# Attention with transposed scores, no row maximum, and both products in 64-column tile pairs

## The chip, the cores and the metric

One core of one Trainium2 chip runs the kernel; the other cores are idle. The metric is the device time of one execution in microseconds (us), the median of several executions. Executions of one kernel agree closely (the kernel before: 1264.5 to 1266.7 over all its runs here), and all timed runs below are of the fast state. Runs that were looked at once, with one time, are marked so; their state is unknown.

Some terms. TensorE multiplies matrices; VectorE, ScalarE and GpSimd work element by element (the exp is ScalarE's); SyncE here only issues DMAs, the transfers between the large memory and the on-chip one. "Issuing" is the time that SyncE spends on starting a transfer. A packet is the piece that one of the core's 16 DMA engines moves at a time. PSUM is where TensorE's products land; a bank edge, in the prediction below, is column 512 or 1024 of a score buffer there, where the kernel cuts two of a head's score products (`cut` in the diff). A slot is one of the buffers that a group of heads is loaded into.

## The reference

```python
B, H, Sq, Sk, D = 16, 32, 192, 1024, 128           # q, k, v: bf16, normal * 0.05

def reference(q, k, v):
    scale = q.shape[-1] ** -0.5
    scores = jnp.einsum("bhqd,bhkd->bhqk", q, k) * scale
    p = softmax(scores, axis=-1)
    return jnp.einsum("bhqk,bhkd->bhqd", p, v)
```

There are 512 independent heads of 192 queries and 1024 keys. K and V are 134.2 MB each, Q and the output 25.2 MB each: 318.8 MB pass through the DMA engines whatever the kernel computes.

## The kernel before

Scores stand with queries on the partitions. A unit is 128 queries of one head, or the last 64 queries of two heads together, so three units make a pair of heads. Per unit: TensorE makes 128x1024 scores; VectorE finds the row maximum and copies the scores out; GpSimd (two units of three) subtracts the maximum, or ScalarE takes the exp; TensorE transposes the result in 8 blocks; ScalarE copies the transposed block out (taking the exp there for two units of three); TensorE multiplies by V. K and Q arrive transposed by the DMA engines, 16 heads at a time, into two slots.

```python
# SyncE: the loads of a group of G = 16 heads (stores cut)
e.dma_start_transpose(kt[:, s], kf[h0:h0 + G].rearrange("g k d -> (g k) d")).then_inc(sxk[s], 16)
e.dma_start_transpose(qt[:, s], qf[h0:h0 + G].rearrange("g k d -> (g k) d")).then_inc(sxq[s], 16)
...
e.dma_start(vs[:, s], vf[h0:h0 + G].rearrange("g (p t) d -> p g t d", t=KT_TILES)).then_inc(svl[s], 16)

# TensorE, per unit: scores, then the transposes of an earlier unit, then V of a still earlier one
ins = pe.matmul(S[:, cs], qt[:, s, x * SQ: x * SQ + 128], kt[:, s, ...512 columns...], start=True, stop=True)
...
for t in range(KT_TILES):
    ins = pe.transpose(PT[:, t, :], X[:, t: SK: KT_TILES], ident[:])
...
ins = pe.matmul(O[:, sl, :], PTS[:, t, :], vs[:, s, x, t, :], start=first, stop=last, ...)
if with_rs:                                        # row sums: one more column, with the same weights
    ins = pe.matmul(O[:, 3, sl: sl + 1], PTS[:, t, :], ones[:, 0:1], ...)
```

## Time and profile before

The kernel before takes 1265.1 us. First the engines' busy time, the DMA's busy tenths and its GB/s in 40 equal slices of the span, its packets, and the chain of waits (shares of the span, followed back from the last instruction), all from the page of the kernel before:

```profile
PE 1234.2 (98%) x20480; PEld 1009.4 (80%) x20480; DVE 1102.0 (87%) x2304; ACT 1048.6 (83%) x1281; POOL 960.4 (76%) x518
...
DMA  9999999999999999999999999999999999999941
GB/s 288 268 261 240 278 280 266 288 270 245 254 269 261 279 233 255 281 275 262 261 230 272 271 276 268 252 251 272 272 267 281 253 263 252 271 261 281 244 118 27
DMA packets 790743, 321.89 MB, mean 255 GB/s; under 512 B 724992, under 2 KB 724992, under 8 KB 790528
...
PE 97%; SPq 1%; DMA 1%; ACT 0%; issue 0%; DVE 0%; ACTq 0%
```

TensorE (PE) looks like the one bound: busy for 98% of the span, and 97% of the chain. The DMA engines are at nine tenths until the last loads have been issued, although nothing in the chain waits for them. Of 790,743 packets, 724,992 are under 512 bytes.

One microsecond at a time (each line: window, then busy time of each engine, granted TensorE clock, busy share of the DMA engines, GB/s), from the windows of the kernel before:

```profile
643.00:644.00 1.00, 1.00 (x21) 0.81 (x18) 0.95 (x2) 1.00 (x3) 1.00 (x2) 1.00 1.28 290
644.00:645.00 1.00, 1.00 (x25) 1.00 (x24) 0.94 (x1) 0.84 (x2) 1.00 (x1) 1.00 1.33 300
645.00:646.00 1.00, 1.00 (x14) 0.77 (x12) 0.66 (x3) 0.58 (x1) 0.20 (x1) 1.00 1.83 34
646.00:647.00 1.00, 1.00 (x22) 0.59 (x20) 1.00 (x4) 0.86 (x1) 0.75 (x1) 1.00 0.55 120
647.00:648.00 1.00, 1.00 (x21) 0.97 (x20) 0.97 (x3) 1.00 (x2) 1.00 (x1) 1.00 1.28 291
666.00:667.00 1.00, 1.00 (x17) 0.77 (x14) 0.97 (x6) 1.00 (x2) 1.00 (x1) 1.00 1.10 418
667.00:668.00 1.00, 1.00 (x21) 0.81 (x18) 0.95 (x2) 1.00 (x3) 1.00 (x2) 1.00 1.01 385
668.00:669.00 1.00, 1.00 (x25) 1.00 (x24) 0.94 (x1) 0.84 (x2) 1.00 (x1) 1.00 1.06 406
```

At 643 us K is being transposed: 290 GB/s, and this figure does not move. At 645 it falls to 34. The trace's packet records have a fetch of 16 KB of instructions (queue 8) starting at 644.6 us; there are 164 such fetches, one every 7.7 us. At 666 V is being copied, at 385 to 418 GB/s, and a fetch that starts at 666.7 us does not stop it. The packet records give the sizes: K and Q move in packets of 256 bytes, V in packets of 2 KB.

| Before, from the trace | |
|---|---|
| K and Q: 159.4 MB at 290 GB/s (worked out) | 550 us |
| V: 134.2 MB at 390 GB/s, the median of the half-microsecond stretches that hold V alone (worked out) | 344 us |
| last V load issued, by the queue's timeline | 1192 us |

### The profile page before, as it was taken

To read this page: it belongs to the slowest core of one execution; us is meant where nothing else is said; L and a number is where in the kernel's file an instruction comes from. 1 tells how busy PE (TensorE), PEld (TensorE's weight loads), DVE (VectorE), ACT (ScalarE), POOL (GpSimd) and SP (SyncE) were. 2 spreads that over 40 slices of the span, in tenths; PEclk is the share of its full clock that TensorE was granted. 3 is DMA by queue.
4 is the path that set the end of the run, shared out by engine and by line. 5 is a ranking of instruction groups with operands and counts; after the bars stand their busy time and mean duration, and the time that the engine had idled before them with its cause. 6 is when DMAs were issued, how large, how long until landed. Compare 5 with 4: busy or idle time off the path is not lost.

```text
span 1263.1 us, 48658 instructions
## 1 busy us (share of the span) xinstructions
PE 1234.2 (98%) x20480; PEld 1009.4 (80%) x20480; DVE 1102.0 (87%) x2304; ACT 1048.6 (83%) x1281; POOL 960.4 (76%) x518
## 2 busy tenths in 40 slices
PE   3999999999999999999999999999999999999997
PEld 1888888888888888888888888888888888888886
DVE  2889888898988989898898988889898898989885
ACT  1888888888888888888888888888888888888886
POOL 2778777777877778787777877777787777878774
PEclk9999999999999999999999999999999999999999
DMA  9999999999999999999999999999999999999941
GB/s 288 268 261 240 278 280 266 288 270 245 254 269 261 279 233 255 281 275 262 261 230 272 271 276 268 252 251 272 272 267 281 253 263 252 271 261 281 244 118 27
DMA packets 790743, 321.89 MB, mean 255 GB/s; under 512 B 724992, under 2 KB 724992, under 8 KB 790528
## 3 DMA queue, kind: packets, MB, share of 16 engines
q1 hardware_dynamic: 790528, 318.78, 108.8%
q8 instruction: 164, 2.69, 0.8%
q14 instruction: 51, 0.42, 0.1%
HBM read 134.22 MB, written 25.17 MB: 126 GB/s over the span
## 4 chain that ended last, share of the span: by engine, by line
PE 97%; SPq 1%; DMA 1%; ACT 0%; issue 0%; DVE 0%; ACTq 0%
PE pt_ps L244 33%; PE o_ps L267 24%; PE s_ps L215 18%; PE o_ps L273 11%; PE s_ps L222 9%; SPq L141 1%; DMA vs<-in_v_dram 1%; PE o_ps L270 1%; PE o_ps L275 1%; SPq L144 0%; PE s_ps L228 0%; ACT x_sb L356 0%; ACT pt_sb L367 0%; DVE ob L330 0%; DVE rinv L327 0%
## 5 line engine op out<-in xcount | busy, mean ns | idle before, releaser
L188 POOL TENSOR_TENSOR x_sb<-ss,nb 128x1024 bf16<-128x1024 f32 x512 | 959.7, 1895 | 288.9 <-PE pt_ps L244 266.8
L300 DVE TENSOR_SCALAR_CACHE_REDUCE ss<-s_ps 128x1024 f32<-128x1024 f32 x768 | 938.5, 1222 | 140.5 <-PE s_ps L215 110.8
L244 PEld LDWEIGHTS pt_ps<-ident,x_sb 128*128 128x128 bf16 x6144 | 487.1, 148 | 203.3 <-issue 105.4
L367 ACT ACTIVATE pt_sb<-pt_ps 128x1024 bf16<-128x1024 bf16 x512 | 521.0, 1018 | 41.9 <-PE pt_ps L244 41.8
L244 PE MATMUL pt_ps<-ident,x_sb 128*128 128x128 bf16 x6144 | 520.7, 228 | 0.2 <-ACT pt_sb L367 0.2
L267 PE MATMUL o_ps<-vs,pt_sb 128*128 128x128 bf16 x4096 | 403.0, 217 | 0.3 <-DMA vs<-in_v_dram 0.3
L369 ACT ACTIVATE pt_sb<-pt_ps 128x1024 bf16<-128x1024 bf16 x256 | 262.1, 1024 | 140.1 <-PE pt_ps L244 140.0
L270 PE MATMUL o_ps<-ones,pt_sb 128*128 128x1 bf16 x4096 | 376.0, 165 | 0.0
L267 PEld LDWEIGHTS o_ps<-vs,pt_sb 128*128 128x128 bf16 x4096 | 352.3, 97 | 0.5 <-DMA vs<-in_v_dram 0.4
L270 PEld LDWEIGHTS o_ps<-ones,pt_sb 128*128 128x128 bf16 x4096 | 340.7, 96 | 0.0
L215 PE MATMUL s_ps<-kt,qt 128*128 128x512 bf16 x1024 | 305.3, 379 | 21.3 <-DMA qt<-in_q_dram 21.0
L356 ACT ACTIVATE x_sb<-ss,nb 128x1024 bf16<-128x1024 f32 x256 | 292.3, 1142 | 23.6 <-DVE ss L300 23.6
L273 PE MATMUL o_ps<-vs,pt_sb 128*64 128x128 bf16 x2048 | 162.3, 222 | 0.0
L275 PE MATMUL o_ps<-vs,pt_sb 128*64 128x128 bf16 x2048 | 162.3, 222 | 0.0
L222 PE MATMUL s_ps<-kt,qt 128*64 128x512 bf16 x512 | 153.2, 381 | 0.6 <-DVE ss L300 0.5
L228 PE MATMUL s_ps<-kt,qt 128*64 128x512 bf16 x512 | 153.2, 381 | 0.0
L330 DVE TENSOR_TENSOR ob<-o_ps,rinv 128x384 bf16<-128x384 f32 x256 | 142.7, 557 | 8.7
L273 PEld LDWEIGHTS o_ps<-vs,pt_sb 128*64 128x64 bf16 x2048 | 121.0, 109 | 17.1
L275 PEld LDWEIGHTS o_ps<-vs,pt_sb 128*64 128x64 bf16 x2048 | 121.0, 109 | 0.0
L215 PEld LDWEIGHTS s_ps<-kt,qt 128*128 128x128 bf16 x1024 | 63.3, 96 | 23.6 <-issue 21.5
L300 DVE DVE_READ_ACCUMULATOR ss<-s_ps 128x1 f32 x768 | 64.0, 83 | 0.0
L356 ACT ACTIVATION_READ_ACCUMULATOR x_sb<-ss,nb 128x1 f32 x256 | 48.9, 191 | 0.0
(11 smaller groups left out, 165.7 us busy)
## 6 DMA issues: line engine op xcount, KB each, us to landing
vs<-in_v_dram SPq DMA_DIRECT2D x32, 4096.0 KB, 15.2
out_dram<-ob SPq DMA_DIRECT2D x32, 512.0 KB, 15.9
out_dram<-ob SPq DMA_DIRECT2D x64, 128.0 KB, 4.9
kt<-in_k_dram SPq DMA_TRANSPOSE x32, 21.4
qt<-in_q_dram SPq DMA_TRANSPOSE x32, 6.6
```

The costliest lines, as they stand in the source:

```text
L188: gp.tensor_tensor(x_sb[:, u % NX, :], ss[:, u % NSS, :], nb[:, u % NSS: u % NSS + 1].to_broadcast([128, SK]), ALU.subtract,).then_inc(s_x ...
L215: ins = pe.matmul(S[:, cs], qt[:, s, x * SQ: x * SQ + 128], kt[:, s, x * SK + 512 * c: x * SK + 512 * c + 512], start=True, stop=True,)
L222: pe.matmul(S[0:64, cs], qt[:, s, a * SQ + 128: a * SQ + 192], kt[:, s, a * SK + 512 * c: a * SK + 512 * c + 512], start=True, stop=True, ...
L244: ins = pe.transpose(PT[:, t, :], X[:, t: SK: KT_TILES], ident[:])
L267: ins = pe.matmul(O[:, sl, :], PTS[:, t, :], vs[:, s, x, t, :], start=first, stop=last, skip_group_check=True)
L270: ins = pe.matmul(O[:, 3, sl: sl + 1], PTS[:, t, :], ones[:, 0:1], start=False, stop=last, skip_group_check=True)
L273: pe.matmul(O[0:64, sl, :], PTS[:, t, 0:64], vs[:, s, a, t, :], start=first, stop=last, skip_group_check=True, tile_position=(0, 0))
L275: ins = pe.matmul(O[64:128, sl, :], PTS[:, t, 64:128], vs[:, s, b, t, :], start=first, stop=last, skip_group_check=True, tile_position=(0, ...
L300: dve.tensor_scalar(ss[:, u % NSS, :], s_ps[u % 2][:], -scale, None, ALU.mult, ALU.min, accum_out=nb[:, u % NSS: u % NSS + 1],).then_inc(s ...
L356: act.activation(x_sb[:, u % NX, :], ss[:, u % NSS, :], ACT_FN.Exp, bias=nb[:, u % NSS: u % NSS + 1], scale=-1.0, accum_out=rs[:, pr % NRS ...
L367: act.activation(pt_sb[:, u % NPT], pt_ps[u % 2][:], ACT_FN.Exp, scale=-1.0).then_inc(s_eva, 1)
L369: act.activation(pt_sb[:, u % NPT], pt_ps[u % 2][:], ACT_FN.Copy).then_inc(s_eva, 1)
```

## The change

The intent is to take work off every compute engine. Scores are made transposed, with keys on the partitions, so the exp's output is already the weights of the second product, and nothing has to be transposed or copied afterwards. With no row maximum there is no pass for it; a check of the row sums runs a general path (the old kernel) if they leave a safe range. The row sum comes from a column of ones beside V. Products are pairs of matmuls on 64-column halves of the array, and the second product of an earlier pair of heads is split between the next heads' scores.

For the ones to stand beside V, V lands in runs of 512 bytes, padded by 64 bytes of ones. For V's layout (key 8p + t on partition p) K is transposed from rows of 8 keys, 2 KB each, and Q from rows of 3 queries. Groups are of 8 heads, in four slots.

```diff
+                    e.dma_start_transpose(
+                        kt[:, s, 0:T * n * 128].rearrange("d (t m) -> d t m", t=T),
+                        kf[h0:h0 + n].rearrange("g (m t) d -> (g m) (t d)", t=T),
+                    ).then_inc(s_kq[s], 16)
+                    e.dma_start_transpose(
+                        qt[:, s, 0:3 * n * 64].rearrange("d (j p) -> d j p", j=3),
+                        qf[h0:h0 + n].rearrange("g (p j) d -> (g p) (j d)", j=3),
+                    ).then_inc(s_kq[s], 16)
...
+                    for i in range(n):
+                        e.dma_start(
+                            vs[:, s, 4 * i: 4 * i + 4, 32:VB],
+                            vf[h0 + i].rearrange("(p u t) d -> p u (t d)", u=4, t=2),
+                        ).then_inc(s_v[s], 16)
...
+                    for t in range(T):                                  # scores of one head
+                        w0 = t * n * 128 + hh * 128
+                        cut = {2: (0, 2, 3), 5: (0, 1, 3)}.get(t, (0, 3))
+                        ...
+                                for x in range(2):
+                                    ins = pe.matmul(
+                                        S[64 * x: 64 * x + 64, c0: c0 + (j1 - j0) * 64],
+                                        kt[:, s, w0 + 64 * x: w0 + 64 * x + 64], mv,
+                                        start=True, stop=True, tile_position=(0, 64 * x))
...
+                    for j, t in order[lo:hi]:                           # second product
+                        for x in range(2):
+                            ...
+                            ins = pe.matmul(
+                                O[64 * x: 64 * x + 64, o0: o0 + 129],
+                                pt[:, (h + x) % NP, t * SQ + j * 64: t * SQ + j * 64 + 64],
+                                vrow[:, c0: c0 + 129], ..., tile_position=(0, 64 * x))
...
+                        if n < NPR:
+                            qk(2 * n)
+                        if n >= 2:
+                            pv(n - 2, 0, 12)
+                        if n < NPR:
+                            qk(2 * n + 1)
+                        if n >= 2:
+                            pv(n - 2, 12, 24)
...
+                    act.activation(pt[:, h % NP, :], s_ps[h % 2][:], ACT_FN.Exp, scale=scale).then_inc(s_exp, 1)
```

(Cut: the row-sum check, the division, the stores in rows of 768 bytes, the general path.)

More of the change, by code (lines that the diff above doesn't have):

```diff
@@ L13, with _only_if, wrap, run @@
 R_W = 2
-def _attention_kernel(nc, q, k, v, out, G=16, NS=2, LAGS=(2, 4, 5, 7), ROUTES=(R_W, R_W, R_EA)):
+def _only_if(redo):
+    def wrap(body):
+        def run(eng):
+            with eng.register() as r:
+                eng.reg_load(r, redo[0:1, 0:1])
+                with eng.If_ne(r, 0):
+                    body(eng)
+        return run
+    return wrap
+def _general_path(nc, q, k, v, out, redo, G=16, NS=2, LAGS=(2, 4, 5, 7), ROUTES=(R_W, R_W, R_EA)):
     B, H, SQ, D = q.shape
@@ L133, in _ @@
         @block.sync
+        @_only_if(redo)
         def _(e):
@@ L176, in _ @@
         @block.gpsimd
+        @_only_if(redo)
         def _(gp):
@@ L197, in _ @@
         @block.tensor
+        @_only_if(redo)
         def _(pe):
@@ L294, in _ @@
         @block.vector
+        @_only_if(redo)
         def _(dve):
@@ L347, in _ @@
         @block.scalar
+        @_only_if(redo)
         def _(act):
@@ L377, in _, with _group_sizes, _attention_kernel, sem @@
                     exp_first(u)
+QK_TILED = True
+RS_LO = 2.0 ** -40
+RS_HI = 2.0 ** 20
+def _group_sizes(NH):
+    if NH >= 32:
+        return [2, 2, 4] + [8] * ((NH - 16) // 8) + [4, 2, 2]
+    return [2] * (NH // 2)
+def _attention_kernel(nc, q, k, v, out, GM=8, NS=4):
+    B, H, SQ, D = q.shape
+    SK = k.shape[2]
+    assert D == 128 and SK == 1024 and SQ == 192, (D, SK, SQ)
+    NH = B * H
+    NPR = NH // 2
+    T = SK // 128
+    scale = float(D) ** -0.5
+    sizes = _group_sizes(NH)
+    assert sum(sizes) == NH
+    first = [sum(sizes[:i]) for i in range(len(sizes))]
+    NG = len(sizes)
+    gof = [g for g in range(NG) for _ in range(sizes[g])]
+    NP = 6
+    NSO = 3
+    VB = 288
+    qf = q.rearrange("b h s d -> (b h) s d")
+    kf = k.rearrange("b h s d -> (b h) s d")
+    vf = v.rearrange("b h s d -> (b h) s d")
+    of = out.rearrange("b h s d -> (b h) s d")
+    with ExitStack() as outer:
+        redo = outer.enter_context(nc.sbuf_tensor("redo", [1, 1], mybir.dt.int32))
+        def sem(name):
+            return outer.enter_context(nc.semaphore(name))
+        s_set = sem("f_set")
+        s_kq = [sem("f_kq%d" % i) for i in range(NS)]
+        s_v = [sem("f_v%d" % i) for i in range(NS)]
+        s_st = [sem("f_st%d" % i) for i in range(NSO)]
+        s_qk = sem("f_qk")
+        s_exp = sem("f_exp")
+        s_pv = sem("f_pv")
+        s_dv = sem("f_dv")
+        s_on = sem("f_on")
+        s_fl = sem("f_fl")
+        with ExitStack() as es:
+            def sb(name, shape, dt):
+                return es.enter_context(nc.sbuf_tensor(name, shape, dt))
+            def ps(name, shape, dt):
+                return es.enter_context(nc.psum_tensor(name, shape, dt))
+            kt = sb("f_kt", [128, NS, T * GM * 128], BF16)
+            qt = sb("f_qt", [128, NS, 3 * GM * 64], BF16)
+            vs = sb("f_vs", [128, NS, GM * 4 + 1, VB], BF16)
+            pt = sb("f_pt", [128, NP, T * SQ], BF16)
+            ob = sb("f_ob", [128, NSO, GM // 2, 3 * D], BF16)
+            rs = sb("f_rs", [128, 2, 3], F32)
+            rinv = sb("f_rinv", [128, NPR * 3], F32)
+            chk = sb("f_chk", [128, NPR * 3], F32)
+            bad = sb("f_bad", [128, 2], BF16)
+            ones = sb("f_ones", [128, 1], BF16)
+            s_ps = [ps("f_s%d" % i, [128, T * SQ], F32) for i in range(2)]
+            o_ps = [ps("f_o%d" % i, [128, 512], F32) for i in range(2)]
+            block = es.enter_context(nc.Block())
+            def kq_cnt(g):
+                return 32 * (g // NS + 1)
+            def v_cnt(g):
+                return 16 * sum(sizes[i] for i in range(g % NS, g + 1, NS))
+            @block.sync
+            def _(e):
+                def loads(g):
+                    s = g % NS
+                    n = sizes[g]
+                    h0 = first[g]
+                    if g >= NS:
+                        e.wait_ge(s_qk, first[g - NS] + sizes[g - NS])
+                    e.dma_start_transpose(
[6 more added lines that the diff above has]
+                    ).then_inc(s_kq[s], 16)
+                    if g >= NS:
+                        e.wait_ge(s_pv, (first[g - NS] + sizes[g - NS]) // 2)
+                    for i in range(n):
[3 more added lines that the diff above has]
+                        ).then_inc(s_v[s], 16)
+                def stores(g):
+                    so = g % NSO
+                    n = sizes[g]
+                    h0 = first[g]
+                    e.wait_ge(s_on, (h0 + n) // 2)
+                    e.dma_start(
+                        of[h0:h0 + n].rearrange("(a x) (p j) d -> (x p) a (j d)", x=2, j=3),
+                        ob[:, so, 0:n // 2, :],
+                    ).then_inc(s_st[so], 16)
+                for g in range(min(NS, NG)):
+                    loads(g)
+                for g in range(NG):
+                    if g + NS < NG:
+                        loads(g + NS)
+                    stores(g)
+                for so in range(min(NSO, NG)):
+                    e.wait_ge(s_st[so], 16 * len(range(so, NG, NSO)))
+            @block.gpsimd
+            def _(gp):
+                for s in range(min(NS, NG)):
+                    gp.memset(vs[:, s, :, 0:32], 1.0).then_inc(s_set, 1)
+                gp.memset(ones[:], 1.0).then_inc(s_set, 1)
+            @block.tensor
+            def _(pe):
+                def qk(h):
+                    g = gof[h]
+                    s = g % NS
+                    n = sizes[g]
+                    hh = h - first[g]
+                    if hh == 0:
+                        pe.wait_ge(s_kq[s], kq_cnt(g))
+                    if h >= 2:
+                        pe.wait_ge(s_exp, h - 1)
+                    S = s_ps[h % 2]
+                    qv = qt[:, s, 0:3 * n * 64].rearrange("d (j r) -> d j r", j=3)
+                    ins = None
+                    for t in range(T):
+                        w0 = t * n * 128 + hh * 128
+                        cut = {2: (0, 2, 3), 5: (0, 1, 3)}.get(t, (0, 3))
+                        for j0, j1 in zip(cut[:-1], cut[1:]):
+                            mv = qv[:, j0:j1, hh * 64: hh * 64 + 64]
+                            c0 = t * SQ + j0 * 64
+                            if QK_TILED:
+                                for x in range(2):
[3 more added lines that the diff above has]
+                                        start=True, stop=True, tile_position=(0, 64 * x))
+                            else:
+                                ins = pe.matmul(
+                                    S[:, c0: c0 + (j1 - j0) * 64],
+                                    kt[:, s, w0: w0 + 128], mv, start=True, stop=True)
+                    ins.then_inc(s_qk, 1)
+                order = [(j, t) for j in range(3) for t in range(T)]
+                def pv(pr, lo, hi):
+                    h = 2 * pr
+                    g = gof[h]
+                    s = g % NS
+                    hh = h - first[g]
+                    if lo == 0:
+                        if pr == 0:
+                            pe.wait_ge(s_set, min(NS, NG) + 1)
+                        if hh == 0:
+                            pe.wait_ge(s_v[s], v_cnt(g))
+                        pe.wait_ge(s_exp, h + 2)
+                        if pr >= 2:
+                            pe.wait_ge(s_on, pr - 1)
+                    O = o_ps[pr % 2]
+                    ins = None
+                    for j, t in order[lo:hi]:
+                        for x in range(2):
+                            b = (hh + x) * 4 + t // 2
+                            vrow = vs[:, s].rearrange("p b c -> p (b c)")
+                            c0 = b * VB + (31 if t % 2 == 0 else 160)
+                            o0 = j * 130 + t % 2
+                            ins = pe.matmul(
+                                O[64 * x: 64 * x + 64, o0: o0 + 129],
+                                pt[:, (h + x) % NP, t * SQ + j * 64: t * SQ + j * 64 + 64],
+                                vrow[:, c0: c0 + 129],
+                                start=t == 0, stop=t == T - 1, skip_group_check=True,
+                                tile_position=(0, 64 * x))
+                    if hi == len(order):
+                        ins.then_inc(s_pv, 1)
+                for n in range(NPR + 2):
+                    if QK_TILED:
+                        if n < NPR:
[6 more added lines that the diff above has]
+                            pv(n - 2, 12, 24)
+                    else:
+                        if n < NPR:
+                            qk(2 * n)
+                            qk(2 * n + 1)
+                        if 1 <= n <= NPR:
+                            pv(n - 1, 0, 24)
+                pe.wait_ge(s_fl, 1)
+                pe.matmul(o_ps[0][0:1, 0:1], ones[:, 0:1], bad[:, 0:1], start=True, stop=False)
+                pe.matmul(o_ps[0][0:1, 0:1], ones[:, 0:1], bad[:, 1:2], start=False, stop=True).then_inc(s_fl, 1)
+            @block.vector
+            def _(dve):
+                cnt = [0]
+                def step(ins):
+                    ins.then_inc(s_dv, 1)
+                    cnt[0] += 1
+                    dve.wait_ge(s_dv, cnt[0])
+                def onorm(pr):
+                    g = gof[2 * pr]
+                    so = g % NSO
+                    a = pr - first[g] // 2
+                    O = o_ps[pr % 2][:, 0:390].rearrange("p (j c) -> p j c", j=3)
+                    ri = rinv[:, 3 * pr: 3 * pr + 3]
+                    dve.wait_ge(s_pv, pr + 1)
+                    step(dve.tensor_copy(rs[:, pr % 2, :], O[:, :, 0]))
+                    step(dve.tensor_tensor(rs[:, pr % 2, :], rs[:, pr % 2, :], O[:, :, 129], ALU.add))
+                    step(dve.reciprocal(ri, rs[:, pr % 2, :]))
+                    if a == 0 and g >= NSO:
+                        dve.wait_ge(s_st[so], 16 * (g // NSO))
+                    dve.tensor_tensor(
+                        ob[:, so, a, :].rearrange("p (j d) -> p j d", j=3),
+                        O[:, :, 1:129],
+                        ri.unsqueeze(2).to_broadcast([128, 3, D]),
+                        ALU.mult,
+                    ).then_inc(s_on, 1)
+                def check(lo, hi, i):
+                    step(dve.tensor_scalar(chk[:, lo:hi], rinv[:, lo:hi], 1.0 / RS_HI, 1.0 / RS_LO, ALU.max, ALU.min))
+                    step(dve.tensor_tensor(chk[:, lo:hi], chk[:, lo:hi], rinv[:, lo:hi], ALU.not_equal))
+                    step(dve.tensor_reduce(bad[:, i: i + 1], chk[:, lo:hi], mybir.AxisListType.X, ALU.max))
+                early = max(NPR - 6, 1)
+                for pr in range(NPR):
+                    onorm(pr)
+                    if pr == early - 1:
+                        check(0, 3 * early, 0)
+                check(3 * early, 3 * NPR, 1)
+                dve.sem_inc(s_fl, 1)
+                dve.wait_ge(s_fl, 2)
+                dve.tensor_copy(redo[0:1, 0:1], o_ps[0][0:1, 0:1]).then_inc(s_fl, 1)
+                dve.wait_ge(s_fl, 3)
+            @block.scalar
+            def _(act):
+                for h in range(NH):
+                    act.wait_ge(s_qk, h + 1)
+                    if h >= NP:
+                        act.wait_ge(s_pv, (h - NP) // 2 + 1)
+                    act.activation(pt[:, h % NP, :], s_ps[h % 2][:], ACT_FN.Exp, scale=scale).then_inc(s_exp, 1)
+        _general_path(nc, q, k, v, out, redo)
```

## The prediction

> **What bounds it now.** The chain of waits is 97% TensorE, and the engine table has TensorE busy 1234 of 1263 us: transposes through the identity (520.7 us), the second product (403 + 162), the row-sum columns (376), the scores (305 + 153). But DMA is a hidden second wall. The 40 slices show DMA at 9 in all but the last two, although loads run two groups ahead and end near 1205 us. In 1 us windows the K/Q transposes run at a flat 290 GB/s (256-byte packets, one per 14 ns on each engine), V at 380-410 GB/s (2 KB packets, 84 ns). Every 7.7 us a 16 KB instruction fetch (164 packets, about 1.04 us each) falls in; during a transpose the rate then drops below 70 GB/s for about 1.5 us. So loads and stores need: transposes 159 MB / 290 = 550 us, V 134 MB / 390 = 344 us, the rest (stores in 256-byte rows, fetch stalls, ends of transposes) about 290 us: some 1180 us in all.
>
> **Removed.** The row-maximum pass (938 us VectorE), the GpSimd subtraction (960), the TensorE transposes (521), their evacuations (783 on ScalarE), the separate row-sum matmuls (376).
>
> **Added, per head.** TensorE: scores of 8 blocks of 192 columns in pairs of 64-column tiles, two cut at a bank edge. The trace's tile pairs start every 55 ns at 128 columns and 220 ns at 512, so I estimate 82 ns at 192: 0.50 + 0.21 us for the cut ones; half a pair's second product, 12 x 56 = 0.68 us. Together 1.39 us, 712 us for 512 heads. ScalarE: one exp of 1536 columns. The trace has 1018 ns for 1024[...]. VectorE about 1.2 us per pair. Compute alone: 730-770 us.
>
> **DMA becomes the bound.** Bytes stay 318.8 MB; 760 us would need 420 GB/s, more than anything sustained here. K rows become 2 KB and Q rows 768 B of contiguous source; V now lands in 512-byte runs; stores in 768-byte rows. [...] Estimate: [...] (550 if packets stay 256 B), V 370-415, stores 75, fetch stalls 110 (about 176 fetches), ends of 136 transposes 50, start and tail 25: 1060-1200. I put the middle at 1040.
>
> **Predicted: 1040 us, 880 to 1240 8 times in 10. Faster by over 2%: 0.87; within 2%: 0.07; slower: 0.06.**
>
> **What would show it.** Right: DMA 9 in all slices; TensorE idle 25-35% with its scores waiting for K/Q loads; [...] packets of 2 KB or 512 B; the DMA queue rarely waiting for compute. Wrong on compute: score pairs over 90 ns, or waits between scores and exp as the main idle. Wrong on DMA: K transposes still in 256-byte packets at 290 GB/s (1150-1260 us), or rates of 390 GB/s throughout (about 870).
>
> **What would make it wrong.** Transposes with a 2 KB source stride slower than 290 GB/s (no gain); V split into slow small packets; fetch stalls that grow with the denser instruction stream; or transposes near the V rate with few stalls, when ScalarE and TensorE set 780-850 us.

Compute alone came to 730-770 us and the DMA sum to 1060-1200 us; the bracket in it is the transposes' 159 MB at the trace's 290 GB/s. The other terms are estimates. Three of them can be worked out again from the trace before: a straight line through its packet times, 14 ns at 256 bytes and 84 ns at 2 KB, gives 24 ns at 512 bytes and 34 at 768, which makes 393 us for V's 262,144 packets on 16 engines and 70 for the stores' 32,768; and 176 fetches of 1.5 us, with 550 us in 1263 of transposes, make 115. From what VectorE's 1.2 us per pair (266.8 us for 256 pairs, or 1.04, in the changed kernel), the ends and the start and tail were worked out is not stated.

## The result and the profile after

The changed kernel is correct and slower: 1335.6 us (1328.0 to 1338.2, 4 runs) against 1265.2, a ratio of 1.0545 with a 95% interval of 1.0516 to 1.0574. Ratios here are the mean time of one kernel's runs over that of the other's in the same rounds, so they are not quite the ratios of the medians quoted.

The same lines of the page, for the changed kernel:

```profile
PE 866.3 (65%) x22530; PEld 835.2 (63%) x22530; DVE 266.8 (20%) x1031; ACT 720.2 (54%) x513; POOL 4.0 (0%) x9
...
DMA  9999999999999999999999999999999999999996
GB/s 202 240 249 230 250 236 251 244 243 259 247 234 243 239 261 251 221 248 234 252 247 226 251 241 247 250 245 258 245 244 245 249 240 260 236 244 255 238 250 150
DMA packets 931344, 321.98 MB, mean 241 GB/s; under 512 B 636224, under 2 KB 931136, under 8 KB 931136
...
SPq 42%; DMA 26%; PE 25%; issue 4%; DVE 3%; DVEq 0%
```

TensorE is now idle for 35% of the span, VectorE for 80%, and the chain has moved to SyncE's issue queue (SPq) and to DMAs. The DMA is at nine tenths in every slice, and the packets have become more, not fewer: 931,344, of which 636,224 are still under 512 bytes. By the packet records these are 622,592 packets of 256 bytes for K and Q, exactly as many as before, 262,144 packets of 512 bytes for V, and 32,768 of 768 for the stores.

Windows of the changed kernel, K's transposes first (517 to 522), then V (525, 526):

```profile
517.00:518.00 1.00, 1.00 (x22) 1.00 (x20) 0.00 (x0) 0.34 (x1) 0.00 (x0) 0.50 1.28 290
518.00:519.00 1.00, 1.00 (x26) 1.00 (x24) 0.04 (x1) 1.00 (x1) 0.00 (x0) 0.59 1.28 291
519.00:520.00 1.00, 1.00 (x40) 1.00 (x36) 0.90 (x4) 0.47 (x2) 0.00 (x0) 1.00 2.63 172
520.00:521.00 1.00, 0.24 (x9) 0.12 (x5) 0.12 (x1) 1.00 (x1) 0.00 (x0) 1.00 0.08 10
521.00:522.00 1.00, 0.29 (x9) 0.29 (x10) 0.00 (x0) 0.09 (x1) 0.00 (x0) 1.00 1.27 289
525.00:526.00 1.00, 0.87 (x30) 0.70 (x26) 0.00 (x0) 1.00 (x2) 0.00 (x0) 1.00 1.13 324
526.00:527.00 1.00, 1.00 (x32) 1.00 (x34) 0.49 (x3) 0.84 (x1) 0.00 (x0) 1.00 1.09 292
```

The transposes still run at 290 GB/s, and still stop at an instruction fetch (519). V comes at about 300 GB/s (324 and 292 in these windows) where it came at 390. The clock of 0.50 in the first line follows a pause: TensorE's timeline has it waiting 5.75 us up to 514.84, and the windows around have the clock at 1.00 until 512, 0.50 from there to 518 and 1.00 from 519. Over the whole run its mean is 0.838, against 0.999 in the kernel before. It is a symptom: in no_reload, below, the same compute with its data at hand has 0.985.

What compute waits for, from the list of waits of the changed kernel, and its exp, from its groups (count, busy us, mean ns, idle before):

```profile
ACT f_pt L657 <- PE f_s L545: 599.5, 226, 10.5
DVE f_ob L628 <- DMA out_dram<-f_ob: 523.1, 62, 16.0
...
PE f_o L578 <- DVE f_ob L628: 353.3, 61, 9.1
```

```profile
L657 ACT ACTIVATE f_pt<-f_s 128x1536 bf16<-128x1536 f32 x512 | 718.9, 1451 | 600.9 <-PE f_s L545 599.5
```

The exp itself takes 1451 ns. VectorE waits 523 us for stores to land before it may overwrite an output buffer, and TensorE waits for VectorE. That reads like a shortage of output buffers, and a first reader might also blame SyncE, whose issues for a group of 8 heads (on average 10.1 us for K, 2.3 for Q, 6.8 for V, 1.0 for the store) fill nearly all of its time. Both are tested below.

### The profile page after: what moved, and what is told of

Same layout as the page of the kernel before. It is cut to its first block, busy times and chain, and to the rows that moved or that the text cites. A ratio compares the mean times of both kernels' runs of the same rounds, so it can differ in the third digit from the quotient of the medians.

```text
span 1333.8 us, 48273 instructions
## 1 busy us (share of the span) xinstructions
PE 866.3 (65%) x22530; PEld 835.2 (63%) x22530; DVE 266.8 (20%) x1031; ACT 720.2 (54%) x513; POOL 4.0 (0%) x9
## 2 busy tenths in 40 slices
DMA packets 931344, 321.98 MB, mean 241 GB/s; under 512 B 636224, under 2 KB 931136, under 8 KB 931136
## 4 chain that ended last, share of the span: by engine, by line
SPq 42%; DMA 26%; PE 25%; issue 4%; DVE 3%; DVEq 0%
SPq L493 30%; DMA out_dram<-f_ob 26%; PE f_o L578 14%; PE f_s L545 11%; SPq L486 7%; SPq L482 5%; DVE f_ob L628 3%; DMA f_qt<-in_q_dram 0%; DVEq L627 0%; DVE f_chk L637 0%; DVE f_rinv L625 0%; DVE f_bad L638 0%; DVE f_rs L623 0%; DVE f_rs L624 0%; PE f_o L604 0%
## 5 line engine op out<-in xcount | busy, mean ns | idle before, releaser
L657 ACT ACTIVATE f_pt<-f_s 128x1536 bf16<-128x1536 f32 x512 | 718.9, 1451 | 600.9 <-PE f_s L545 599.5
L578 PE MATMUL f_o<-f_vs,f_pt 128*64 128x129 bf16 x12288 | 541.9, 243 | 403.5 <-DVE f_ob L628 353.3
L578 PEld LDWEIGHTS f_o<-f_vs,f_pt 128*64 128x64 bf16 x12288 | 483.7, 125 | 423.5 <-issue 422.8
L545 PE MATMUL f_s<-f_qt,f_kt 128*64 128x192 bf16 (+2 forms) x10240 | 514.2, 250 | 55.3 <-issue 30.7
L545 PEld LDWEIGHTS f_s<-f_qt,f_kt 128*64 128x64 bf16 x10240 | 417.8, 122 | 66.1 <-issue 39.2
L628 DVE TENSOR_TENSOR f_ob<-f_o,f_rinv 128x384 bf16<-128x384 f32 x256 | 142.7, 558 | 529.7 <-DMA out_dram<-f_ob 523.1
L623 DVE COPY f_rs<-f_o 128x3 f32<-128x3 f32 x256 | 40.6, 159 | 512.3 <-PE f_o L578 512.3
L625 DVE RECIPROCAL f_rinv<-f_rs 128x3 f32<-128x3 f32 x256 | 45.2, 176 | 8.9
L624 DVE TENSOR_TENSOR f_rs<-f_rs,f_o 128x3 f32<-128x3 f32 x256 | 40.4, 158 | 8.9
L520 POOL MEMSET f_vs<- 128x1056 bf16 x4 | 3.7, 979 | 0.3 <-POOLq L683 0.3
```

The lines of the kernel that those rows point to most:

```text
L520: gp.memset(vs[:, s, :, 0:32], 1.0).then_inc(s_set, 1)
L545: ins = pe.matmul(S[64 * x: 64 * x + 64, c0: c0 + (j1 - j0) * 64], kt[:, s, w0 + 64 * x: w0 + 64 * x + 64], mv, start=True, stop=True, til ...
L578: ins = pe.matmul(O[64 * x: 64 * x + 64, o0: o0 + 129], pt[:, (h + x) % NP, t * SQ + j * 64: t * SQ + j * 64 + 64], vrow[:, c0: c0 + 129], ...
L623: step(dve.tensor_copy(rs[:, pr % 2, :], O[:, :, 0]))
L624: step(dve.tensor_tensor(rs[:, pr % 2, :], rs[:, pr % 2, :], O[:, :, 129], ALU.add))
L625: step(dve.reciprocal(ri, rs[:, pr % 2, :]))
```

## The experiments

Theory D: the DMA stream is the bound. Compute has become fast, but the same bytes in no better packets now set the time, and V's packets got worse. Theory F, a part of it: instruction fetches stall the transposes. The rivals are C (the new compute chain is slow by itself), S (SyncE's issue queue is the bound), O (too few output buffers) and P (compute and DMA disturb each other in on-chip memory). Seventeen kernels ran.

### no_reload: the compute alone

```diff
-                    if g + NS < NG:
-                        loads(g + NS)
                     stores(g)
```

(The load counts that compute waits for become those of the first load; groups are all of 8.)

> K, Q and V are loaded for the first four groups of 8 heads only; every later group computes on the old data, so the result is wrong on purpose. Stores stay. Theory D (the DMA stream is the bound, and compute waits for it): the time falls to 740-800 us, ScalarE busy 700-740 us of it, over 90%, and the granted TensorE clock returns to 0.95 or more. Rival C (the compute chain itself, scores - exp - second product - division, has grown slow): the time stays above 1200 us.

Measured: 753.0 us (one look). The page of no_reload:

```profile
PE 706.8 (94%) x22530; PEld 703.6 (94%) x22530; DVE 272.5 (36%) x1031; ACT 699.6 (93%) x513; POOL 4.0 (1%) x9
```

Theory D is right in its first half, and C falls: the changed compute takes 753 us when its data is there, which is the "730-770 us" of the prediction.

### dma_only: the DMA stream alone

All compute is cut; a load waits for the load that had its slot before, and stores wait for nothing but a cleared buffer.

> The same loads and stores with no compute at all (the output is zeros, wrong on purpose); a load waits only for the load that had its slot before. Theory D: 1150-1260 us: the packets at the rates seen in the changed kernel need 549 + 418 + 68 = 1034 us, plus the ends of 136 transposes at about 1 us; only the instruction-fetch stalls (about 160 us by my count) are gone. Rival C: under 1000 us.

Measured: 1199.3 us (one look). The loads and stores alone, with no engine computing, take 90% of the changed kernel's time. While they stay as they are, no change to the compute can bring the kernel below this. Worked out from the rates above: 550 us for K and Q at 290 GB/s, 447 for V at 300, 67 for stores at some 370 (the packet records of dma_k_plain, below), which leaves 135 us beside the packets' own time (about 115 with the rates of dma_only's own records, 291 for V and 344 for the few stretches of stores alone). In its windows the rate dips for about a microsecond at changes from one transfer to the next (148, 211 and 208 GB/s at 602, 604 and 613 us); that all of this time lies there is not shown.

### v_act: V issued from another queue

```diff
-                    for i in range(n):
+                    for i in range(n if g < NS else 0):
...
+                        for x in left:                       # ScalarE, after the exp that frees the place
+                            act.wait_ge(s_pv, ...)
+                            act.dma_start(vs[:, s, 4 * x: 4 * x + 4, 32:VB], ...).then_inc(s_v[s], 16)
```

> The 512 V loads but those of the first groups are issued from ScalarE's queue instead of SyncE's. Rival S (SyncE's one queue of issues is the bound: 9.7 + 2 + 7 + 0.8 us per group of 8 heads add up to all of its time): some 5-8 us of 20.9 per group go, so the time falls to 900-1050 us. Theory D (the 16 engines' packets are the bound[...]): within 4% of 1335 us, and the transposes' issues get longer by what V gave up.

Measured: 1519.3 us, a ratio of 1.198 to the kernel before. Both were wrong on the number. Rival S falls: with 8 of the 11 issues of a group gone SyncE's time did not shrink, and the kernel got 14% longer than the change. From SyncE's timeline (start, duration in us), first in v_act, then in the changed kernel:

```profile
519.38 24.54 SPq L482 DMA_TRANSPOSE f_kt<-in_k_dram  x1
543.97 4.93 SPq L486 DMA_TRANSPOSE f_qt<-in_q_dram  x1
...
549.57 14.81 SPq L482 DMA_TRANSPOSE f_kt<-in_k_dram  x1
```

```profile
509.84 9.44 SPq L482 DMA_TRANSPOSE f_kt<-in_k_dram  x1
519.32 2.60 SPq L486 DMA_TRANSPOSE f_qt<-in_q_dram  x1
```

K's transposes now take 13 to 25 us to issue where they took 9 to 13 in the changed kernel. V's packets (512 bytes, the other queue) and the transposes' are now in flight together, and the packet records show what that costs: half-microsecond stretches that hold both, away from fetches, add up to 644 us at a mean of 227 GB/s (18.5 us in the changed kernel, where V alone has 272, and K and Q alone too), and stretches under 20 GB/s beside a fetch add up to 144 us (64.5 there). No run varied the mixing by itself.

### out_bufs: twice the output buffers

```diff
-    NSO = 3
+    NSO = 6
```

> Six output buffers in place of three. Rival O (VectorE waits 523 us for stores to land before it may overwrite an output buffer, and TensorE 353 us for VectorE): these waits go and the time falls by over 10%. Theory D: the same time within 1%; the waits move to the scores, for K and Q loads, or to V.

Measured: 1361.6 us, a ratio of 1.074 to the kernel before and 2% longer than the change, so D's "within 1%" is missed, on the other side. Rival O falls. From the list of waits of out_bufs:

```profile
ACT f_pt L657 <- PE f_s L545: 635.3, 234, 10.9
...
PE f_s L545 <- DMA f_qt<-in_q_dram: 373.1, 68, 10.1
```

The 523 us of VectorE for stores are gone, and TensorE waits 373 us for Q's loads instead (24 before). As for the other 2%: in the packet records of the profiled executions, half-microsecond stretches under 20 GB/s beside an instruction fetch add up to 95.5 us here and to 64.5 in the changed kernel, which is about the difference. Why the fetches cost more here stays open.

### dma_fetch and dma_fetch_few: the stream, and a TensorE that only fetches

```diff
+            @block.tensor
+            def _(pe):
+                pe.wait_ge(s_set, NS + 3)
+                for _i in range(22528):                     # few: range(5632), 448 columns
+                    pe.matmul(s_ps[0][:, 0:112], ones[:], ones[:, 0:112], start=True, stop=True)
```

> The loads and stores alone, as in dma_only (1199 us), plus a TensorE that waits for nothing and feeds nobody: 22528 matmuls, as many as the changed kernel has, of 112 columns, all on one small tile. So there are about 178 instruction fetches, but no other engine, no waits on compute, and hardly any traffic of compute. Output zeros, wrong on purpose. Theory F (instruction fetches stall the transposes): 1280-1340 us, some 0.5-0.8 us lost per fetch. Rival P (compute and DMA get in each other's way in on-chip memory, or compute's waits hold the loads up): within 2% of 1199 us.

> As dma_fetch (1349 us), but TensorE's idle-running work is done by a quarter of the matmuls, each of 448 columns: TensorE is as busy, with about 45 fetches in place of 178. Theory F: the cost of fetches falls with their number, to some 37 us above dma_only's 1199: 1225-1250 us. Rival P (a running TensorE, whatever it fetches, slows the DMA): stays at 1320-1350 us. Output zeros, wrong on purpose.

Measured: 1348.5 and 1239.2 us (one look each). The first is a little over F's range (1280-1340), the second inside it. The line of instruction fetches (packets, MB, share of the engines' time) in the page of dma_only, then of dma_fetch and of dma_fetch_few:

```profile
q8 instruction: 1, 0.02, 0.0%
```

```profile
q8 instruction: 178, 2.92, 0.9%
```

```profile
q8 instruction: 46, 0.75, 0.3%
```

The three points lie on a line: 1 fetch 1199, 46 fetches 1239, 178 fetches 1349, that is 0.89 us for each of the first 45 more, and 0.84 over all 177. TensorE's matmuls were as busy in both (1111 and 1067 us, though weights were loaded a quarter as often in the second), and P, which had the second stay above 1320, falls as the main cause. The packet records of dma_fetch tie the loss to the fetches in time. Over the 89 fetches that start in the middle of a transpose, the mean rate is 289 GB/s before the fetch, 38 to 53 from 0.75 to 1.75 us after its start, and 266 again at 2.25 us. Over the 64 that start while V flows it stays above 250 in the same time. So it is a transpose that a fetch stalls, and a fetch that falls on V costs little. With 178 fetches and no real compute the stream takes what the changed kernel takes (1336), so nothing else of the compute is needed to explain its time.

### untiled: fewer instructions in the changed kernel

```diff
-                            if QK_TILED:
+                            if False:
```

(The order of the products stays; only the scores use 128-column weights, so their instructions are half as many.)

> The scores with full 128-column weights in place of tile pairs, in the same order: 17408 matmuls and as many weight loads in place of 22528, so about 136 fetches for 178. Theory F: 25-45 us less than the changed kernel, 1290-1310 us. Rival P: within 1% of 1335 us, or longer, since weights of 128 columns and of 64 alternate.

Measured: 1312.7 us (ratio 1.0382), 23 us less. 138 fetches in place of 178 at 0.84 us each make 34. The direction is F's, the size two thirds, and the time just over F's range. (What one change between weights of 128 and of 64 columns costs was measured later: about 0.11 us, from k_on_pe and the two runs after it.)

### v_2kb: V in rows of 2 KB

```diff
-                            vs[:, s, 4 * i: 4 * i + 4, 32:VB],
-                            vf[h0 + i].rearrange("(p u t) d -> p u (t d)", u=4, t=2),
+                            vr[:, s, i, :],
+                            vf[h0 + i].rearrange("(p t) d -> p (t d)", t=T),
...
+                    gp.tensor_copy(                          # GpSimd, per pair of heads
+                        vs[:, pr % NVP, 0:8, 32:VB],
+                        vr[:, s, hh: hh + 2, :].rearrange("p h (b c) -> p (h b) c", c=256),
+                    ).then_inc(s_vc, 1)
```

> V lands in rows of 2 KB, as in the kernel before, and GpSimd, idle otherwise, copies it into the layout with the columns of ones. Theory D with the rates of the two traces: V takes 65536 packets of 84 ns in place of 262144 of 26 ns on 16 engines, 344 for about 425 us, so some 80 us less: 1240-1270 us. If the rows of V do not matter: within 1% of 1335 us. If GpSimd's copy (no trace of it yet) took over 5 us per pair of heads, the time would be longer.

Measured: 1271.2 us (ratio 1.0052), 64 us less, just over D's range. The two rates, 300 and 390 GB/s, would have given 103 us; by the packet records V's stretches ran at a median of about 330 in this kernel. GpSimd's copy took 1.90 us per pair, and TensorE's weight loads waited 16 us for it in all.

### before_v512: that one part in the kernel before

```diff
-        vs = sb("vs", [128, NS, G, KT_TILES, 128], BF16)
+        vs = sb("vs", [128, NS, G, KT_TILES // 2, 288], BF16)
...
-                e.dma_start(
-                    vs[:, s], vf[h0:h0 + G].rearrange("g (p t) d -> p g t d", t=KT_TILES)
-                ).then_inc(svl[s], 16)
+                for i in range(G):
+                    e.dma_start(
+                        vs[:, s, i, :, 32:288], vf[h0 + i].rearrange("(p u t) d -> p u (t d)", u=4, t=2)
+                    ).then_inc(svl[s], 16)
```

> The kernel before with one part of the change alone: V in 512-byte runs, one DMA per head. Theory D: the kernel before was itself next to its DMA stream's limit (loads ended 60 us before the end), so 80 us more of V makes it slower: 1290-1330 us, with TensorE now waiting for loads. Rival: TensorE, busy 98%, hides it: within 1% of 1265 us.

Measured: 1334.9 us, ratio 1.0554 (1.0539 to 1.0569), a little over the top of the range. The old kernel with nothing of the change but V's landing is as slow as the changed kernel. (The edit also makes one DMA per head out of one per group; v_2kb has one per head too and got its 64 us back, so the length of the runs is what counts.) The chain of waits in the page of before_v512:

```profile
PE 57%; SPq 29%; DMA 9%; issue 3%; ACT 1%; DVE 0%; ACTq 0%
```

It was 97% TensorE. So the kernel before stood next to two walls at once: V's loads, longer by about 103 us at the two rates, moved its time by 70 us although TensorE had been busy 98% of the span.

### k_old_order: the source rows of K

```diff
-                        kf[h0:h0 + n].rearrange("g (m t) d -> (g m) (t d)", t=T),
+                        kf[h0:h0 + n].rearrange("g k d -> (g k) d"),
...
-                                    kt[:, s, w0 + 64 * x: w0 + 64 * x + 64], mv,
+                                    kt[:, s, w0 + 512 * x: hh * 1024 + 512 * x + 512: T], mv,
```

> The changed kernel with K transposed from its old source order: 128-column rows that follow each other, in place of 128 columns out of rows of 1024; TensorE then reads its weights with a step of 8. The step of the prediction that is in doubt: 'K rows become 2 KB[...]'. If the wide rows had helped the transposes at all, this is slower than 1335 us by up to 60 us. If they did nothing (both traces show 256-byte packets at 290 GB/s): within 1.5% of 1335 us. If they hurt: faster.

Measured: 1343.8 us, ratio 1.0615, 0.7% from the changed kernel. The packets are the same 622,592 of 256 bytes, at 290 GB/s. The wide rows of K gained about 0.7%, if anything (Q's were not tried alone). This was the step of the prediction in doubt.

### dma_k_plain: the stream with K not transposed

```diff
-                    e.dma_start_transpose(
-                        kt[:, s, 0:T * n * 128].rearrange("d (t m) -> d t m", t=T),
-                        kf[h0:h0 + n].rearrange("g (m t) d -> (g m) (t d)", t=T),
+                    e.dma_start(
+                        kt[:, s, 0:T * n * 128].rearrange("p (g x) -> p g x", g=n),
+                        kf[h0:h0 + n].rearrange("g (p t) d -> p g (t d)", t=T),
```

> The DMA stream alone (dma_only, 1199 us) with K as a plain copy in rows of 2 KB; Q still transposed, V still in 512-byte runs. If the transpose itself is what K costs: 463 us of K become 336 us at V's old rate, and up to half of the 161 us that dma_only lost besides go, 990-1075 us. If K were bound by something else (HBM, the queue): above 1150 us. Output zeros, wrong on purpose.

Measured: 970.6 us (one look), 229 us below dma_only and below the expected range. The GB/s by slices in the page of dma_only and in that of dma_k_plain:

```profile
GB/s 206 263 265 269 260 264 273 266 280 268 262 276 265 268 277 263 272 275 261 277 271 269 276 268 277 269 267 279 270 269 279 270 262 267 266 276 265 274 277 191
```

```profile
GB/s 278 322 329 341 316 340 338 323 343 331 331 342 313 343 335 326 344 328 327 340 321 345 333 329 343 325 331 338 324 343 330 332 343 313 344 335 326 343 328 253
```

K's packets alone explain 134.2 MB / 290 less 134.2 MB / 390, or 119 us; the other 110 is time beside the packets that went away with K's transposes (by subtraction; V is not in it, since its stretches run at 291 GB/s in both kernels by the packet records). Transposing K by DMA costs the stream more than any other part that was tried. The run changes the packet's size together with the transposing, so which of the two is slow is not shown; the plain 256-byte stores at the end of the kernel before ran at only about 200 GB/s.

### big_groups and dma_big: half as many groups

```diff
-        return [2, 2, 4] + [8] * ((NH - 16) // 8) + [4, 2, 2]
+        return [2, 2, 4, 8] + [16] * ((NH - 32) // 16) + [8, 4, 2, 2]
...
-def _attention_kernel(nc, q, k, v, out, GM=8, NS=4):
+def _attention_kernel(nc, q, k, v, out, GM=16, NS=2):
```

> The changed kernel with groups of 16 heads in two slots, as in the kernel before, in place of 8 in four: 36 pairs of transposes in place of 68, and as many fewer stores. Theory D with a cost at each switch between transposes and other packets (dma_only lost 161 us apart from its packets' own time, about 2.4 us per group): 40-75 us less, 1260-1295 us. Rival: the number of groups does not matter, within 1% of 1335 us, or two slots starve compute and it gets longer.

> The DMA stream alone with groups of 16 in two slots. big_groups gained only 8 us where 40-75 were expected. If each switch of kind of packet costs time but compute's waits ate the gain in big_groups: 1130-1160 us against dma_only's 1199. If the number of groups costs the stream nothing: within 1.5% of 1199. Output zeros, wrong on purpose.

Measured: big_groups 1327.2 us (ratio 1.0486), only 8 us less; dma_big 1163.8 us (one look), 36 us below dma_only, just over its range. The number of groups does cost the stream time, about 1.2 us for each of the 30 groups fewer (68 became 38; the expectation miscounted them as 36). With compute and only two slots most of that gain is lost: the list of waits of big_groups has TensorE waiting for V, an entry that the changed kernel's list does not have.

```profile
PE f_o L578 <- DMA f_vs<-in_v_dram: 259.0, 32, 10.3
```

### combo: three repairs together

> Three repairs together: V in 2 KB rows with GpSimd's copy, untiled scores, groups of 16 in two slots. If the three costs add up (65 + 23 + 40 to 75): 1175-1215 us, 4-7% faster than the kernel before. If they overlap or the two slots starve: 1220-1260 us.

Measured: 1198.0 us, ratio 0.9478 (0.9458 to 0.9498): correct, and 5.2% faster than the kernel before. The single gains measured (64, 23 and 8) add up to 95 us, and together they give 138. So the repairs help each other; which ones do, and how, was not followed up.

### k_on_pe: K transposed by TensorE

```diff
-                    e.dma_start_transpose(kt..., kf...).then_inc(s_kq[s], 16)
+                    e.dma_start(
+                        kn[:, s, 0:n, :], kf[h0:h0 + n].rearrange("g (p t) d -> p g (t d)", t=T),
+                    ).then_inc(s_kl[s], 16)
...
+                    for t in range(T):
+                        ins = pe.transpose(k_ps[h % 2][:, t, :], kn[:, s, hh, t * 128: t * 128 + 128], ident[:])
...
+                    dve.tensor_copy(kt[:, h % NKT], k_ps[h % 2][:]).then_inc(s_ev, 1)
```

(With v_2kb's V and untiled scores. A head's scores are made in two halves of 768 columns, in two PSUM buffers of 1024 columns in place of 1536, and K has two buffers of 1024 bf16 columns there.)

> The changed compute with the slow part of its DMA stream taken away: K lands untransposed in 2 KB rows like V, TensorE transposes it (8 per head) and VectorE copies the result out; V as in v_2kb; scores in halves to make room in PSUM. Only Q is still transposed by DMA. Theory D: packets need 336 + 336 + 87 + 68 = 827 us, and fetches now seldom hit a transpose; TensorE about 1.9 us per head, 970 us, ScalarE 1024 x 0.81 = 830[...]: 960-1080 us. If the DMA rate was not what the transposes cost: above 1150 us.

Measured: 1186.9 us, ratio 0.9376 (0.9360 to 0.9392): 6.2% faster than the kernel before, but outside the range of 960-1080. The number lies in the branch that was to speak against D, so it decides nothing; the page does. The busy line of its page, and TensorE's order in its timeline (start, duration, what, count):

```profile
PE 1160.3 (98%) x21506; PEld 955.9 (81%) x21506; DVE 603.0 (51%) x1543; ACT 830.2 (70%) x1025; POOL 486.3 (41%) x266
```

```profile
600.48 0.51 PE L583 MATMUL f_s<-f_qt,f_kt 128*128 128x192 bf16 x5
600.92 0.54 PE L608 MATMUL f_o<-f_vs,f_pt 128*64 128x129 bf16 x12
601.38 0.62 PE L560 MATMUL f_k<-f_ident,f_kn 128*128 128x128 bf16 x8
601.84 0.50 PE L583 MATMUL f_s<-f_qt,f_kt 128*128 128x192 bf16 x5
602.27 0.54 PE L608 MATMUL f_o<-f_vs,f_pt 128*64 128x129 bf16 x12
...
603.64 0.62 PE L560 MATMUL f_k<-f_ident,f_kn 128*128 128x128 bf16 x8
```

DMA is no longer the bound; TensorE is (96% of the chain of waits). From one group of K's transposes (601.38) to the next (603.64) is 2.26 us per head. Five score matmuls of 768 columns together take 0.43 us to the start of the next group, 602.27 less 601.84, where 55 ns per 128 columns, the pace of tile pairs in the kernel before, gives 0.33. ScalarE took 810 ns for an exp of 768 columns, 830 us in all as expected. (Here a copy of K took 686 ns, and VectorE was busy 603 us in all.)

### k_on_pe_tiled and k_on_pe_grouped: the changes of tile width

k_on_pe_tiled does the transposes and scores in 64-column pairs too, so the width never changes. k_on_pe_grouped changes the order alone:

```diff
                     for half in range(2):
                         if h < NH:
                             qk(h, half)
-                        if h >= 4:
-                            lo = 12 * (h % 2) + 6 * half
-                            pv(h // 2 - 2, lo, lo + 6)
+                    if h >= 4:
+                        lo = 12 * (h % 2)
+                        pv(h // 2 - 2, lo, lo + 12)
```

> k_on_pe (1187 us, TensorE 98% busy, 2.25 us per head where its matmuls' columns add up to 1.85) with everything in 64-column tile pairs, so that TensorE never changes between 128-column and 64-column weights, which it does four times a head in k_on_pe at about 0.1 us each by its trace. If the changes cost it that: 960-1040 us, until DMA at some 340 GB/s (940 us) is the limit. If not, within 2% of 1187 us.

> k_on_pe (1187 us) with the order alone changed: both halves of a head's scores together, then all of that head's share of the second product, so that TensorE changes between 128-column and 64-column weights twice a head in place of four times, with the same instructions as k_on_pe. k_on_pe_tiled reached 1.81 us per head between its stalls against 2.25 in k_on_pe, so two changes of width cost some 0.2 us per head: 1065-1105 us. If the order costs waits for exp or for the score buffers instead: 1150-1190 us.

Measured: k_on_pe_tiled 1342.9 us (ratio 1.0604), k_on_pe_grouped 1132.3 us (ratio 0.8941, 0.8918 to 0.8963). The first missed by 300 us. Between its stalls it does reach 1.81 us per head, 0.45 less than in k_on_pe for four changes of width fewer, or 0.11 us for each. But windows like these come again and again:

```profile
608.00:609.00 1.00, 1.00 (x41) 1.00 (x37) 0.50 (x2) 0.89 (x2) 0.46 (x1) 1.00 1.10 414
...
610.00:611.00 1.00, 0.00 (x0) 0.00 (x0) 0.00 (x0) 0.00 (x0) 0.00 (x0) 1.00 0.45 26
```

In the second no engine works at all, and the profile names nothing that TensorE waits for; by its matmul records there are 139 pauses of over 0.4 us, 305 us in all. It has 30,722 matmuls and 244 fetches, against 21,506 and 172 in k_on_pe, which has 13 such pauses and 13 us. The records show what it waited for: 129 of the 139 pauses end 1.2 to 1.6 us after a 16 KB instruction fetch has ended (a fetch comes every 5.5 us, so chance would give 7%), and 132 of the 138 stretches from one resumption to the next hold a multiple of 256 TensorE instructions, to within 2, where a fetch comes for every 252 (61,444 matmuls and weight loads over 244 fetches). That fits a TensorE that had run out of instructions; no run varied this by itself, and why the fetches came late was not tried.

k_on_pe_grouped runs the same instructions as k_on_pe with two changes of width per head in place of four, and is 55 us faster. TensorE's timeline of it:

```profile
602.27 0.62 PE L560 MATMUL f_k<-f_ident,f_kn 128*128 128x128 bf16 x8
602.73 0.83 PE L583 MATMUL f_s<-f_qt,f_kt 128*128 128x192 bf16 x10
603.49 0.88 PE L608 MATMUL f_o<-f_vs,f_pt 128*64 128x129 bf16 x24
604.30 0.62 PE L560 MATMUL f_k<-f_ident,f_kn 128*128 128x128 bf16 x8
```

One head takes 2.03 us, 0.23 less than in k_on_pe: about 0.11 us for each change of width saved, as in k_on_pe_tiled. That is 117 us for 512 heads. Only 55 came, and the time missed the range of 1065-1105; 42 us of the rest are new pauses like those above (49 of them, 55 us in all, against 13 us in k_on_pe). It is the fastest kernel and correct: 10.6% faster than the kernel before, 15% faster than the change.

## Why the prediction was wrong

- **"DMA becomes the bound"** was right, and the runs show it directly: compute alone 753 us, DMA alone 1199.
- **"Compute alone: 730-770 us"** was right (753). ScalarE's exp took 1.451 us in the changed kernel, and it was busy 700 us in no_reload. TensorE was put at 712 us and was busy 707 there.
- **The failed step is the estimate of the DMA sum, first of all its term for the transposes.** The term was lower than the bracket, "550 if packets stay 256 B". The wide source rows of K and Q did not widen the packets: 622,592 of 256 bytes before and after, at 290 GB/s in both. What came was the 550 us of the bracket, and k_old_order shows that the rows of K make about 0.7% of difference, if any.
- **V, "370-415"**, needed about 447 at the 300 GB/s of 512-byte packets. The effect in the kernel was measured twice: 64 us back with 2 KB rows, 70 us added to the old kernel by 512-byte runs.
- **"Fetch stalls 110" and "ends of 136 transposes 50"** were measured as about 136 us (the changed kernel less dma_only; dma_fetch has 149) and about 135 us of the stream alone beside its packets.
- Together: 550 + 447 + 67 + 135 + 136 = 1335 us, where the prediction's sum was 1060-1200: the cut term and (370 to 415) + 75 + 110 + 50 + 25. (The 135 and 136 are what the measured times leave, so that the sum closes shows nothing by itself; the terms do.) Every term but the stores was too low. The packets of 256 bytes alone would not have broken the range: with 550 and 415 the prediction's own list gives 1225, and it named 1150-1260 for this case. The other 110 us are V (32), the fetches (26) and the time beside the packets (135 where ends, start and tail had 75), less 8 of stores. And the middle, 1040, lay below every sum of its own list, which begins at 1060.
- The wrong "faster" follows from this. The kernel before needed "some 1180 us" of DMA by the prediction's own count. The change took nothing off that stream but wider stores, and narrowed V. The gain in compute went off the critical path whole.
- **"Scores waiting for K/Q loads"** was wrong as a sign: with three output buffers the wait shows on stores instead, 523 us. With six it shows on Q's loads. Here the place of the wait told which buffer was scarcest, not what bounds the kernel.

## What to carry to other kernels

Before compute is made faster, count what the DMA stream needs by itself, kind of packet by kind of packet, at the rates of the trace; a kernel whose chain of waits is 97% TensorE can still stand next to that wall (here shorter runs of V alone cost it 70 us). Then run the stream with the compute taken out and the compute with the loads taken out: two runs told here that the stream set the time and not the compute; the other rivals needed runs of their own. When the stream is the wall, look at what lands in short runs (here V's 512-byte runs, 64 us of the changed kernel) or is transposed by DMA (here K, 229 us of the stream alone), and try moving that work to an engine that has just become idle.
